# A transformer block in one kernel: squares moved from ScalarE to GpSimd, two more joint units, GpSimd's queue run by a clock

## The chip, the core and the metric

The kernel runs on one core of one Trainium2 chip. A core has five engines that run their own instruction queues and meet only through semaphores: TensorE (PE in the profile; its weight loads are PEld), VectorE (DVE), ScalarE (ACT), GpSimd (POOL) and SyncE (SP), which issues the DMAs. PE writes its results to PSUM, eight banks of 128 x 512 fp32; DVE and ACT read them there. The metric is the device time of one execution in microseconds (us), the median of several runs.

## What is computed

A pre-layernorm block: attention, then a gated feed-forward network, both with a residual. S = 2048 rows, D = 512, H = 32 heads of 16, F = 1792, all in bf16.

```python
def _A_ref(x, wqkv, wo):
    qkv = (x @ wqkv).reshape(B, S, 3, H, Dh) ...
    scores = jnp.einsum("bhqd,bhkd->bhqk", q, k) * (Dh ** -0.5)
    p = _softmax(scores, axis=-1)
    o = jnp.einsum("bhqk,bhkd->bhqd", p, v)
    return o... @ wo

def _B_ref(x, w_gate, w_up, w_down):
    return (_gelu(x @ w_gate) * (x @ w_up)) @ w_down

h = x + _A_ref(_layernorm(x), A_wqkv, A_wo)
h2 = h + _B_ref(_layernorm(h), B_w_gate, B_w_up, B_w_down)
```

The softmax takes the maximum of every row of scores, and the scores are 32 x 2048 x 2048 numbers: they are computed twice, once for the maxima and once, transposed, for the exponentials.

## The kernel before

**Units, groups and ticks.** Four heads (a slot) and 256 query rows make a unit; there are 64, and eight units (all heads for the same rows) make a group. The main loop at the end of the kernel function runs over ticks, 16 to a unit. In pass 1 a tick computes a pair of 128 x 512 score blocks (`p1_pair`, L825) and DVE reduces the pair to two maxima per row in one instruction (`p1_consume`, L840). Pass 2 follows 24 ticks behind (`P2_START`): two tiles a tick (`p2_tile`, L904), each 128 keys twice x 256 queries, and one Exp on ACT for each (`p2_consume`, L933). The exponentials wait in a ring of buffers (PTM, PTE, PTG) until `item_pv` (L947) multiplies them with the values.

**From the maxima to pass 2.** After ticks 9 and 13 of a unit `negm_part`, and after its end `negm_pre` and `negm_post` (`unit_end`), let GpSimd combine the maxima (some 17 small instructions, L851 to L876), SP transpose them (STG), and GpSimd add them to the queries (L888), so that the second scores come out with the maximum taken off. That addition is put `ADDX` = 3 ticks after the unit's end.

**Joint units.** For the units in `JOINT` (11 of them) one tick less is needed. ACT gets the difference of two score blocks (`item_diff`, L1022, L1024) and keeps its Relu in RB (L1027); DVE adds that Relu to the other block while it takes the maximum (L837, two instructions in place of one at L840), which gives the maximum of both. Tick 14 (`J_GONE`) of such a unit is left out, and pass 2's two tiles of that tick are made up on odd ticks (`behind`). `joint_prep` puts the two differences of a unit into the list `extra`; `J_PREP` says at which tick, from tick 160 at the earliest.

**Everything else goes in between.** `Dense` holds the other work of PE as generators: projections (`item_projT`, `item_projV`), values (`item_pv`), output projections (`item_oproj`), and gate, up and down of the feed-forward network. Once a tick `Dense.piece` lets the current item go on, or starts one: an extra that is due, an item of `prio` that is due, an extra, or the first of `ready`. Whether it may start hangs on `act_lag`, the planner's own account of ACT's backlog (each Exp adds 0.478, each tick takes off 1.135), and on `tight()`, which is true at the end of a joint unit. An item returns how many products of 512 columns it was worth; the loop fills a tick of pass 1 up to two with idle products (`dummy`, L1380). All of this is planned while the program is built; on the chip only the order on each engine and the semaphores count.

**Norm of the second half.** When a group's heads are done, SP transposes the rows (`post_onT`), `item_oproj` multiplies with wo, ACT adds the residual and sums the row (L1094), and two ticks later ACT squares the row with a second sum (`sq`, L1101), when its account of backlog is low. GpSimd then computes the norm (`ln2_from_sums`, `ln2_finish`, L1111 to L1125), and SP transposes it (`post_hnT`), which is done in ticks 5 to 13 of a unit alone (`clear`). Then the seven pairs of gate and up start. For each pair ACT takes both out of PSUM, GpSimd computes the inner polynomial (L1158 to L1160), ACT the Tanh (L1148; `later` waits until the backlog is under `LAG_TH` = 0.2 plus 0.02 for each tick already waited), and GpSimd the rest (L1156, L1157, L1212). The eighth group's norm and network come after both passes, in `tail_b`.

**GpSimd's queue.** `PoolStream` holds GpSimd's optional work. Each tick gives it a budget of 1.19 (at most 1.25), and the next instruction is put in the program when the budget covers its cost. `charge` keeps `t`, the time at which GpSimd would be done by the planner's clock (`TICK` = 1.135 a tick); before the change only the Tanh's placing reads it. The reciprocals of the softmax sums (`inv`, L981) are kept out of some ticks.

Of the kernel before, what the change touches and what calls it, by code (L numbers as in the profile page):

```python
# [222 lines left out]
ADDX = 3  # L223
# [7 lines left out]
TANH_LAG = 2  # L231
SLOPE = 0.02
JOINT = (12, 14, 17, 20, 25, 28, 33, 36, 41, 44, 49)
# [5 lines left out]
LAG_TH = 0.2  # L239


def bass_sequential_preLN__mha_block__geglu_ffn__prompt_kernel(nc, A_x, A_wqkv, A_wo, B_x, B_w_gate, B_w_up, B_w_down, out):
    dbg = None
    with ExitStack() as es:
# [54 lines left out]
        hn_sb = OnT[:].rearrange("p q c s -> p q (c s)")  # L299
        xres = at("xres", [128, 4, D], BF16)  # L300
# [223 lines left out]
        class Dense:  # L524
# [27 lines left out]
            def piece(self):  # L552
                if self.single and self.pause > 0:
                    return 0
                while True:
                    if self.gen is None:
                        lim = 10 ** 9
                        for it in self.prio:
                            lim = min(lim, max(it[3], self.now))
                        self.prio.sort(key=lambda it: it[3])  # L560
                        if self.extra and self.now >= 16 * self.extra[0][1][0] + 2:
                            self._start(self.extra.pop(0))
                        elif self.prio and (not self.single or self.prio[0][3] <= self.now):
                            self._start(self.prio.pop(0))
                        elif self.extra and not tight() and act_lag[0] <= LAG_EXTRA and self.now + 2 <= lim and not (self.ready and self.ready[0][0] is item_up):
                            self._start(self.extra.pop(0))
                        elif self.ready and (not self.single or ((act_lag[0] <= (-1 if tight() else LAG_START) or force[0] or self.ready[0][0] not in (item_gate, item_up)) and startable(self.ready[0], lim - self.now) and self.ready[0][3] <= self.now and self.now + self.ready[0][2] + PAUSE - 1 <= lim)):
                            self._start(self.ready.pop(0))
                        else:
                            return 0  # L570
# [46 lines left out]
        class PoolStream:  # L617

            def __init__(self):
                self.q = []  # L620
                self.budget = 0.0
                self.t = 0.0
            def add(self, ops, then=None):
                for i, (cost, fn) in enumerate(ops):
                    self.q.append((cost, fn, then if i == len(ops) - 1 else None))
                if force[0] or not ticking[0]:
                    self.run(True)
            def spend(self, cost):
                self.budget -= cost
            def charge(self, took, ready=0.0):  # L630
                self.t = max(self.t, TICK * dense.now, ready) + took
                return self.t
            def run(self, flush=False):
                while self.q and (flush or self.budget >= min(self.q[0][0], 1.0) or (self.q[0][1].__name__ == 'inv' and dense.now % 16 == 0)):
                    if not flush and self.q[0][1].__name__ == 'inv' and dense.now % 16 in (1, 2, 3, 12, 13, 14, 15):
# [242 lines left out]
        def negm_post(ui):  # L878
# [6 lines left out]
            def add():  # L885
                pool.spend(0.7)
                pool.charge(0.63, st_end[0] + 2.75)
                P.op("pool", lambda e: e.tensor_tensor(out=q_ap, in0=q_ap, in1=STG[:, par, :], op=ALU.add), reads=[("STG", par), ("qT", slot, c, hf)], writes=[("qT", slot, c, hf)])  # L888
                q_ready.add(ui)
            defer(ADDX + (ui == NU - 1), add)  # L890
# [126 lines left out]
        def item_diff(b, ui, g):  # L1017
# [11 lines left out]
            return 3  # L1029
# [33 lines left out]
        def post_onT(gi, k):  # L1063
# [7 lines left out]
            dense.add(item_oproj, gi, k, front=True, est=3, not_before=dense.now + 5)  # L1071
# [11 lines left out]
        def item_oproj(b, gi, k):  # L1083
            gp, t = gi % 2, 2 * gi + k
            hh = g_h(gi, k)
            for hc in range(4):
                P.op("pe", lambda e, hc=hc: e.matmul(pbank[:, b, :], OnT[:, k, hc, :], wo_sb[:, hc, :], start=(hc == 0), stop=False),
                     reads=[("OH", k), "wo"], writes=[("pb", b)], sig=False)
                if hc == 1:
# [5 lines left out]
                 reads=[("pb", b)], writes=[("h", gp, k), ("hsum", t)])  # L1095
            def sq():
# [7 lines left out]
            defer(2, sq)  # L1104
# [279 lines left out]
        def unit_end(ui):  # L1384
# [3 lines left out]
            negm_post(ui)  # L1388

# [5 lines left out]
        J_PREP = {max(160, 16 * (J_[i - 1] if i else 0) + 12): J_[i] for i in range(len(J_))}  # L1395
# [7 lines left out]
        while True:  # L1403
# [94 lines left out]
            if w_pieces and tick % 16 in (7, 9, 11, 13):  # L1498
# [40 lines left out]
```

## Time and profile before

| | us |
|---|---|
| median of 3 runs (1234.56 to 1235.47) | 1234.57 |
| the profiled execution | 1234.76 |
| its span, first to last instruction | 1232.9 |

The profile is one execution. Its page gives each engine's busy time and share of the span; views of the trace give the instructions in order of time (the timeline: start, length, engine, line, operation, operands, count of the instructions merged, and in brackets the idle time before it and what ended it), and busy time in chosen windows. Instructions of ACT and DVE overlap at their ends, so a full engine's pace is read from start to start, and a busy share of 99% can hide short waits. The granted TensorE clock is 1.00 in every window.

### The profile page before, as it was taken

What the parts mean: (1) busy time and instruction counts of PE and PEld (TensorE: products, weight loads), DVE (VectorE), ACT (ScalarE), POOL (GpSimd) and SP (SyncE); (2) the same over time, 40 slices, a digit from 0 to 9 for tenths busy, and PEclk for the clock granted to TensorE, in tenths of its full rate; (3) what the DMA queues carried; (4) which work ended last, traced back from release to release, by engine and by line L of the source; (5) the groups of instructions that cost most, each with busy time, mean ns of one, the idle gap of its engine ahead of it and who ended that gap; (6) DMA issues with size and microseconds to landing.
All of it is one profiled execution on the core that took longest, in us unless ns stands there. A gap on an engine that the chain in (4) does not pass through costs nothing.

```text
span 1232.9 us, 31298 instructions
## 1 busy us (share of the span) xinstructions
PE 1102.3 (89%) x12444; PEld 427.4 (35%) x12580; DVE 1179.1 (96%) x1107; ACT 1195.2 (97%) x2437; POOL 784.4 (64%) x1624
## 2 busy tenths in 40 slices
PE   7898888899999988999889998899889898888898
PEld 3233222233333333333333343333333333233335
DVE  8999999999999999999999999999999999999933
ACT  7899999999999999999999999999999999999993
POOL 8567873566756587466755677366765687347850
PEclk9999999999999999999999999999999999999999
DMA  5111113200011000100011000110001000100000
GB/s 152 27 34 30 33 50 116 76 10 9 8 27 25 8 10 9 39 13 8 11 25 27 8 8 11 25 27 8 9 10 38 14 9 8 35 17 10 8 19 14
DMA packets 68657, 31.53 MB, mean 26 GB/s; under 512 B 53920, under 2 KB 67488, under 8 KB 68512
## 3 DMA queue, kind: packets, MB, share of 16 engines
q1 hardware_dynamic: 68512, 29.52, 9.5%
q8 instruction: 101, 1.65, 0.6%
q14 instruction: 44, 0.36, 0.1%
HBM read 11.80 MB, written 2.10 MB: 11 GB/s over the span
## 4 chain that ended last, share of the span: by engine, by line
ACT 50%; DVE 30%; POOL 8%; PE 7%; issue 3%; DMA 1%; POOLq 0%; DVEq 0%
DVE PM L840 29%; ACT PTM L933 29%; ACT PTG L933 8%; ACT PTE L933 4%; PE pbank L1220 2%; ACT g_sb L669 1%; POOL th_sb L1158 1%; PE pbank L904 1%; ACT u_sb L669 1%; DMA STG<-ST 1%; PE pbank L825 1%; ACT th_sb L1148 1%; POOL LINV L981 1%; PE pbank L1168 1%; POOL GUT L1212 1%
## 5 line engine op out<-in xcount | busy, mean ns | idle before, releaser
L840 DVE TENSOR_REDUCE PM<-pbank 128x2 f32<-128x1024 f32 x1002 | 1141.4, 1213 | 8.8 <-PE pbank L904 5.1
L933 ACT ACTIVATE PTM<-pbank 128x512 bf16<-128x512 f32 x1357 | 730.3, 718 | 3.4 <-PE pbank L904 0.6
L904 PE MATMUL pbank<-QT,KT 32*128 32x256 bf16 x4096 | 512.2, 273 | 16.2 <-ACT PTM L933 6.0
L825 PE MATMUL pbank<-KT,QT 32*128 32x512 bf16 x2026 | 390.1, 384 | 29.9 <-DVE PM L840 11.3
L1380 PE MATMUL pbank<-ones_bf,ident 128*128 128x512 bf16 x697 | 217.3, 383 | 56.2 <-ACT PTM L933 29.1
L933 ACT ACTIVATE PTG<-pbank 128x512 bf16<-128x512 f32 x407 | 227.7, 716 | 1.2 <-PE pbank L904 0.2
L825 PEld LDWEIGHTS pbank<-KT,QT 32*128 32x128 bf16 x2026 | 97.7, 90 | 369.8 <-DVE PM L840 133.2
L904 PEld LDWEIGHTS pbank<-QT,KT 32*128 32x128 bf16 x4096 | 171.2, 92 | 85.2 <-ACT PTM L933 46.5
L933 ACT ACTIVATE PTE<-pbank 128x512 bf16<-128x512 f32 x236 | 139.1, 718 | 0.8
L947 PE MATMUL pbank<-PTM,VA 128*17 128x256 bf16 x2776 | 125.4, 274 | 1.5
L981 POOL TENSOR_TENSOR LINV<-OBT,negone 128x8 f32<-128x8 bf16 x62 | 103.4, 1668 | 0.0
L1380 PEld LDWEIGHTS pbank<-ones_bf,ident 128*128 128x128 bf16 x796 | 46.0, 97 | 140.1 <-ACT PTM L933 90.0
L1158 POOL TENSOR_TENSOR th_sb<-g_sb 128x512 f32<-128x512 f32 x49 | 50.9, 1040 | 41.6 <-ACT g_sb L669 41.6
L947 PEld LDWEIGHTS pbank<-PTM,VA 128*17 128x17 bf16 x2776 | 60.0, 89 | 45.7 <-issue 29.6
L1168 PE MATMUL pbank<-hnT_l,wg_sb 128*128 128x256 bf16 x448 | 67.0, 275 | 3.6
L1168 PE MATMUL pbank<-hnT_l,wu_sb 128*128 128x256 bf16 x448 | 67.1, 275 | 2.3
L868 POOL TENSOR_TENSOR MX<-PM,MX 128x8 f32<-128x8 f32 x64 | 12.8, 200 | 86.6 <-DVE PM L840 86.3
L1160 POOL TENSOR_TENSOR th_sb<-th_sb,g_sb 128x512 f32<-128x512 f32 x49 | 62.1, 1267 | 3.4
L1212 POOL TENSOR_TENSOR GUT<-th_sb,u_sb 128x512 bf16<-128x512 f32 x49 | 61.8, 1267 | 2.5
L1157 POOL TENSOR_TENSOR th_sb<-th_sb,g_sb 128x512 f32<-128x512 f32 x49 | 62.2, 1269 | 1.4
L888 POOL TENSOR_TENSOR QT<-QT,STG 128x256 bf16<-128x256 bf16 x64 | 42.7, 668 | 30.5 <-DMA STG<-ST 30.5
L1220 PE MATMUL pbank<-wd_sb,GUT 128*128 128x512 bf16 x210 | 57.3, 382 | 3.4 <-ACT OB L669 1.3
(163 smaller groups left out, 1096.0 us busy)
## 6 DMA issues: line engine op xcount, KB each, us to landing
QKS<-QKS SPq DMA_DIRECT2D x27, 112.0 KB, 2.1
x_sb<-in_A_x_dram SPq DMA_DIRECT2D x4, 512.0 KB, 5.5
xres<-in_A_x_dram SPq DMA_DIRECT2D x16, 128.0 KB, 2.3
out_dram<-out_sb SPq DMA_DIRECT2D x16, 128.0 KB, 1.7
wg_sb<-in_B_w_gate_dram SPq DMA_DIRECT2D x4, 448.0 KB, 3.6
wu_sb<-in_B_w_up_dram SPq DMA_DIRECT2D x4, 448.0 KB, 3.9
wd_sb<-in_B_w_down_dram SPq DMA_DIRECT2D x3, 512.0 KB, 4.2
STG<-ST SPq DMA_TRANSPOSE x64, 2.3
```

What stands on the lines that cost most here:

```text
L825: P.op("pe", lambda e, g=g, b=b: e.matmul(pbank[:, b, :], QT[32 * g:32 * g + 32, c, slot, 128 * qt:128 * qt + 128], KT[32 * g:32 * g + 32, ...
L840: P.op("dve", lambda e: e.tensor_reduce(out=PM[:, par, qt, kc, g:g + 2], in_=pbank[:, b:b + 2, :], axis=AX.X, op=ALU.max), reads=[("pb", b ...
L904: P.op("pe", lambda e, kt=kt, i=i: e.matmul(pbank[:, b, 256 * i:256 * i + 256], KT[32 * g:32 * g + 32, slot, 128 * kt:128 * kt + 128], QT[ ...
L933: P.op("act", lambda e, b=b, pi=pi: e.activation(out=PTt(pi), in_=pbank[:, b, :], func=ACT.Exp), reads=[("pb", b)], writes=[("PT", pi)], e ...
L947: P.op("pe", lambda e, g=g, kt=kt, pi=pi, i=i: e.matmul(pbank[32 * g:32 * g + 17, b, 0:256], VA[:, kt, 4 * slot + g, :], PTt(pi)[:, 256 * ...
L981: P.op("pool", lambda e: e.tensor_tensor(out=li, in0=o4[:, :, :, 16], in1=negone[:, 0:8].rearrange("p (q h) -> p q h", q=2), op=ALU.pow), ...
L1157: o(1.27, lambda e: e.tensor_tensor(out=ts_, in0=ts_, in1=gs, op=ALU.mult), [("th", par), ("g", par)])], then=done)
L1158: pool.add([o(1.04, lambda e: e.tensor_tensor(out=ts_, in0=gs, in1=gs, op=ALU.mult), [("g", par)], dE), o(0.62, lambda e: e.tensor_scalar( ...
L1168: P.op("pe", lambda e, dc=dc, fc=fc, i=i: e.matmul(pbank[:, b, 256 * i:256 * i + 256], w[:, dc, 128 * fc:128 * fc + 128], hT[:, dc, :], st ...
L1212: P.op("pool", lambda e: e.tensor_tensor(out=o_ap, in0=shp(ts_), in1=shp(us), op=ALU.mult), reads=[("th", par), ("u", par)], writes=o_keys ...
L1220: P.op("pe", lambda e: e.matmul(pbank[:, b, :], GUT[:, fc, 128 * k:128 * k + 128], wd_sb[:, fc, :], start=first, stop=last), reads=[("GUT" ...
L1380: P.op("pe", lambda e: e.matmul(pbank[:, b, :], ident[:], ones_bf[:, 0:512], start=True, stop=True), reads=["ident", "ones_bf"], writes=[( ...
```

## The change

Squares: for groups 0 to 5 the sum of squares is made by GpSimd: two products of 256 columns, their sum, and seven additions that halve the row, the last into `hsq`. `HQ` lies over the buffer that holds the square's output before; `HR` is new. The seventh group (`GL - 1`) keeps ACT's Square.

Two more units are joint (5 and 9), with their differences prepared from tick 60. GpSimd's queue is run by its clock from tick 64 on (`fits`): the next instruction is put in the program unless GpSimd is planned busy beyond the next tick by over 0.8, or the instruction would straddle, by over 0.3, the time at which the maxima or the addition come due. The addition is put a tick later from tick 64 on. A difference counts as one product instead of three, so that an idle one goes beside it. Differences start at a backlog of 0.05 (0.3 in the last six ticks before their unit), Tanhs at 0.05; an output projection is held back for up to six ticks while the backlog is over 0.1, and the second tile's is due one tick later; from tick 56 on projections too wait for the backlog. The weights of the feed-forward network are loaded at five ticks of a unit instead of four.

```diff
-ADDX = 3
+ADDX = 4
+CLOCK = 64
+AHEAD, OVER = 0.8, 0.3
-JOINT = (12, 14, 17, 20, 25, 28, 33, 36, 41, 44, 49)
+JOINT = (5, 9, 12, 14, 17, 20, 25, 28, 33, 36, 41, 44, 49)
-LAG_TH = 0.2
+LAG_TH = .05
...
+        HQ = at("HQ", [128, 2, 256], FP32, cur[0] - 2048)
+        HR = at("HR", [128, 256], FP32)
...
+                        elif self.prio and self.prio[0][0] is item_oproj and self.prio[0][3] <= self.now < self.prio[0][3] + 6 and act_lag[0] > 0.1:
+                            return 0
...
-                        elif self.extra and not tight() and act_lag[0] <= LAG_EXTRA and ...
+                        elif self.extra and not tight() and act_lag[0] <= (LAG_EXTRA if self.now >= 16 * self.extra[0][1][0] - 6 else 0.05) and ...
-                        elif self.ready and (... or force[0] or self.ready[0][0] not in (item_gate, item_up)) and ...
+                        elif self.ready and (... or force[0] or self.ready[0][0] not in (item_gate, item_up) and (self.ready[0][0] is not item_projT or self.now < 56)) and ...
...
+            def fits(self, took):
+                t0 = max(self.t, TICK * dense.now)
+                if t0 > TICK * (dense.now + 1) + AHEAD:
+                    return False
+                due = [TICK * (dense.now // 16 * 16 + 15) + 2.35 if dense.now < 16 * NU else 1e9]
+                if self.add_due:
+                    due.append(st_end[0] + 2.75)
+                return not any(t0 < d < t0 + took - OVER for d in due)
...
-            defer(ADDX + (ui == NU - 1), add)
+            defer(ADDX - (dense.now < CLOCK) + (ui == NU - 1), add)
...
             P.op("act", lambda e: e.activation(out=RB[:, g, :], in_=pbank[:, b, :], func=ACT.Relu), ...)
             y_left[ui] -= 1
-            return 3
+            return 1
...
-            dense.add(item_oproj, gi, k, front=True, est=3, not_before=dense.now + 5)
+            dense.add(item_oproj, gi, k, front=True, est=3, not_before=dense.now + 5 + k)
...
+            def squares():
+                hq, w = HQ[:, k, :], [("OH", k)]
+                ops = []
+                o = lambda cost, fn, reads, writes: ops.append((cost, lambda: P.op("pool", fn, reads=reads, writes=writes)))
+                o(0.63, lambda e: e.tensor_tensor(out=hq, in0=hh[:, 0:256], in1=hh[:, 0:256], op=ALU.mult), [("h", gp, k)], w)
+                o(0.63, lambda e: e.tensor_tensor(out=HR[:], in0=hh[:, 256:512], in1=hh[:, 256:512], op=ALU.mult), [("h", gp, k)], ["HR"])
+                o(0.63, lambda e: e.tensor_tensor(out=hq, in0=hq, in1=HR[:], op=ALU.add), w + ["HR"], w)
+                n = 128
+                while n > 1:
+                    o(0.2 + 0.0017 * n, lambda e, n=n: e.tensor_tensor(out=HQ[:, k, 0:n], in0=HQ[:, k, 0:n], in1=HQ[:, k, n:2 * n], op=ALU.add), w, w)
+                    n //= 2
+                o(0.2, lambda e: e.tensor_tensor(out=hsq[:, t:t + 1], in0=HQ[:, k, 0:1], in1=HQ[:, k, 1:2], op=ALU.add), w, [("hsq", t)])
+                pool.add(ops + ln2_from_sums(gi, k, t), then=lambda: defer(2, lambda: clear(lambda: post_hnT(gi, k))))
...
-            defer(2, sq)
+            defer(2, sq if gi == GL - 1 else squares)
...
-        J_PREP = {max(160, 16 * (J_[i - 1] if i else 0) + 12): J_[i] for i in range(len(J_))}
+        J_PREP = {max(60, 16 * (J_[i - 1] if i else 0) + 12): J_[i] for i in range(len(J_))}
...
-            if w_pieces and tick % 16 in (7, 9, 11, 13):
+            if w_pieces and tick % 16 in (5, 7, 9, 11, 13):
```

## The prediction

> **What bounds the kernel now.** I read the page first, then a table of windows cut at the group boundaries, then the timeline of VectorE (DVE) alone, then that of ScalarE (ACT).
>
> ```profile
> span 1232.9 us, 31298 instructions
> PE 1102.3 (89%) x12444; PEld 427.4 (35%) x12580; DVE 1179.1 (96%) x1107; ACT 1195.2 (97%) x2437; POOL 784.4 (64%) x1624
> ...
> ACT 50%; DVE 30%; POOL 8%; PE 7%; issue 3%; DMA 1%; POOLq 0%; DVEq 0%
> ```
>
> Two engines are nearly full and the chain that ends last changes between them. The profiled execution took 1234.76 us (1.9 around its span); the sum below is made against it. The median of the runs is 1234.57, 0.2 less.
>
> ```profile
> 219.37:363.50 144.13, 129.48 (x1501) 49.58 (x1515) 142.71 (x135) 143.91 (x300) 93.89 (x200) 1.00 0.09 20
> 363.50:508.37 144.87, 131.96 (x1520) 51.12 (x1535) 143.83 (x133) 144.44 (x302) 93.52 (x198) 1.00 0.07 16
> 508.37:653.40 145.03, 131.41 (x1517) 50.46 (x1534) 143.81 (x134) 144.57 (x300) 93.18 (x198) 1.00 0.07 16
> 653.40:798.27 144.87, 131.25 (x1517) 50.42 (x1532) 143.66 (x133) 144.40 (x300) 93.10 (x198) 1.00 0.07 16
> 798.27:943.30 145.03, 131.76 (x1522) 50.90 (x1539) 143.78 (x134) 144.41 (x299) 92.66 (x197) 1.00 0.08 17
> 943.30:1089.30 146.00, 130.12 (x1531) 49.79 (x1545) 145.34 (x130) 144.87 (x298) 91.85 (x194) 1.00 0.07 17
> 1089.30:1180.48 91.18, 80.24 (x960) 32.70 (x968) 90.88 (x81) 91.13 (x190) 70.81 (x140) 1.00 0.06 12
> ```
>
> Each row is a group of eight units (the last: five); the columns after the length are busy time and instructions of PE, PEld, DVE, ACT and POOL, then the granted clock. GpSimd (POOL) is busy 93 of 145 us. DVE's own pace shows in its timeline:
>
> ```profile
> 484.29 0.68 DVE L837 CUSTOM_DVE_ANT_0 OA<-pbank,OA 128x512 f32<-128x512 f32 x1
> ...
> 484.90 0.68 DVE L837 CUSTOM_DVE_ANT_0 OA<-pbank,OA 128x512 f32<-128x512 f32 x1
> ...
> 485.51 27.62 DVE L840 TENSOR_REDUCE PM<-pbank 128x2 f32<-128x1024 f32 x24
> 513.32 2.36 DVE L840 TENSOR_REDUCE PM<-pbank 128x2 f32<-128x1024 f32 x2 [0.19 <-PE pbank L904]
> 515.83 22.71 DVE L840 TENSOR_REDUCE PM<-pbank 128x2 f32<-128x1024 f32 x20
> ...
> 1009.98 145.15 DVE L840 TENSOR_REDUCE PM<-pbank 128x2 f32<-128x1024 f32 x128 [0.26 <-PE pbank L904]
> 1155.40 25.08 DVE L840 TENSOR_REDUCE PM<-pbank 128x2 f32<-128x1024 f32 x22 [0.27 <-PE pbank L904]
> ```
>
> A reduce that lasts 1.21 overlaps the next: 128 of them in 145.15 are one per (145.15 - 1.21) / 127 = 1.133 us. A joint instruction at L837 takes 0.61 (484.29 to 484.90 to 485.51). A group with two joint units has 124 reduces and four joint instructions, so DVE's floor is 124 x 1.133 + 4 x 0.61 = 142.9, and the rows say 144.9 to 145.0: about 2.1 us of stall in each of four groups. By the same count the first row (three joint units, floor 141.9) has 2.2, the sixth (none, 145.0) 1.0 and the last (80 reduces, 90.6) 0.5: **11.9 us of stall in all**. The stalls end on PE's L904, which waits for a PSUM bank, which ACT gives free: they are ACT's backlogs. Reduces end at 1155.40 + 25.08 = 1180.48; the 52 us after that are a tail.
>
> **The change part by part.**
>
> *Two more joint units* (5 and 9). Each takes out two reduces and adds two joint instructions: 2 x 1.133 - 2 x 0.61 = 1.05, for two units **-2.1**. They give ACT 2 x 2 Relus. ACT's prices, by starts in its timeline:
>
> ```profile
> 505.09 2.08 ACT L933 ACTIVATE PTG<-pbank 128x512 bf16<-128x512 f32 x4
> 507.00 0.67 ACT L1094 ACTIVATE xres<-pbank 128x512 bf16<-128x512 f32 x1
> 507.47 0.27 ACT L1094 ACTIVATION_READ_ACCUMULATOR xres<-pbank 128x1 f32 x1
> 507.57 1.16 ACT L933 ACTIVATE PTG<-pbank 128x512 bf16<-128x512 f32 x2
> 508.52 2.16 ACT L933 ACTIVATE PTM<-pbank 128x512 bf16<-128x512 f32 x4
> 510.48 0.71 ACT L1101 ACTIVATE OnT<-xres 128x512 bf16<-128x512 bf16 x1
> 511.00 0.27 ACT L1101 ACTIVATION_READ_ACCUMULATOR OnT<-xres 128x1 f32 x1
> 511.10 2.13 ACT L933 ACTIVATE PTM<-pbank 128x512 bf16<-128x512 f32 x4
> ...
> 92.74:219.37 126.63, 108.06 (x1277) 35.95 (x1290) 126.63 (x113) 124.55 (x251) 81.69 (x151) 1.00 0.21 63
> ```
>
> Four exps fill 505.09 to 507.00, 0.478 each; a Relu of the same size is put at that. The stage of units 4 to 10 (the last row) has 251 ACT instructions in 126.63: at 0.478 some 120, so 6.6 are free though the busy column hides it. Two joint units need 2 x (1.05 + 0.96) = 4.0 of that, if the rule that projections after tick 56 wait for a small backlog spreads them. Bounds -2.1 and 0 (all given back as stalls); I take -2.1.
>
> *Squares off ACT.* Twelve of fourteen go. One is 510.48 to 511.10, 0.62 with its read of the accumulator: 7.4 us of ACT, 1.24 in each of six groups. What of it is on the path is read where it stands: 24 reduces from 485.51 and two from 513.32 should take 27.2 and 2.27, and take 27.81 and 2.51, so 0.86 is lost around the two output projections (507.00 to 507.57: 0.57 each, which stay) and the two squares. I take 0.5 per group, **-3.0**; bounds 0 (the backlog is then the projections') and -0.86 x 6 = -5.2.
>
> *What GpSimd gets*: eleven instructions for each square.
>
> ```profile
> 503.86 0.20 POOL L855 TENSOR_TENSOR MX<-PM,MX 128x8 f32<-128x8 f32 x1 [3.73 <-DVE PM L840]
> 504.15 0.23 POOL L856 TENSOR_SCALAR MX<-MX 128x8 f32<-128x8 f32 x1
> ...
> 512.23 0.40 POOL L985 TENSOR_TENSOR Otok<-OBT,LINV 128x128 bf16<-128x128 bf16 x1
> 513.63 0.67 POOL L888 TENSOR_TENSOR QT<-QT,STG 128x256 bf16<-128x256 bf16 x1
> 518.63 0.77 POOL L1125 TENSOR_SCALAR OnT<-xres,rstd,nmr 128x512 bf16<-128x512 bf16 x1
> ...
> L1212 POOL TENSOR_TENSOR GUT<-th_sb,u_sb x7: 1264/1267/1268, 539.5 to 625.9; 128x512 bf16<-128x512 f32 x7
> L1094 ACT ACTIVATE xres<-pbank x2: 614/640/665, 649.5 to 652.0; 128x512 bf16<-128x512 f32 x2
> ```
>
> Three of 256 columns by L888 (3 x 0.67), one of 128 by L985 (0.40), seven of 64 down to 1 between those and L855 (about 0.22): 3.9 us by durations; starts are 0.29 apart where the row L855 says 0.20, so 4.9 with that gap. Twelve cost 47 to 59 of the 448 us that GpSimd is idle. The two tiles of a group make its norm some 10 us longer, less the gap of 3.7 at 503.86 and its like; so the feed-forward of the group starts about 8 late, or 16 where the transposes that follow the norm, which SP's queue gets in ticks 5 to 13 of a unit alone, miss a window (seven ticks). Its last product stood at 625.9 and the next output projection at 649.5, 23 us later, which hides it: 0. Without that cover the next group's products would be pushed by what is over, one for one. The seventh group, the last whose network runs in the loop, keeps its squares on ACT.
>
> The Trainium skill, "Perfetto Trace Analysis", section "GPSIMD Engine Instruction", says to time GpSimd by starts, not by reported spans; here spans give 3.9 a tile and starts 4.9, and as both lie under the cover the sum is the same by either.
>
> *GpSimd by a clock of its queue; the addition at L888 a tick later.* The order on GpSimd changes, the work does not. Behind the addition wait the gelu products of the queue; it waits for a transpose, and a tick (1.133) later more of that wait is used. The exps that need it start eight ticks after the unit. 0; in the tail, where one product of 1.27 could come ahead of it, up to +1.3.
>
> *Gates* (tanh at a backlog of 0.05 instead of 0.2, differences at 0.05, an output projection held back over 0.1, a tile's projection a tick later). They only put ACT work off to calmer ticks. The stall not counted yet is 11.9 - 5.2 = 6.7. Bounds 0 and -6.7; by nearness to the lower end (the instructions stay) **-1.0**.
>
> *A filler beside each difference.*
>
> ```profile
> 403.58 0.39 PE L825 MATMUL pbank<-KT,QT 32*128 32x512 bf16 x2
> ...
> 404.02 0.39 PE L1022 MATMUL pbank<-KT,QT 32*128 32x512 bf16 x1
> 404.25 0.37 PE L1024 MATMUL pbank<-KT,QN 32*128 32x512 bf16 x1
> 404.55 0.39 PE L825 MATMUL pbank<-KT,QT 32*128 32x512 bf16 x2
> ```
>
> A tick with a difference takes PE 0.97 (403.58 to 404.55); one more product of 0.23 (404.02 to 404.25) makes 1.20, 0.07 over the reduce. 26 of them: up to +1.8; the next ticks take it up, so 0. The weights' pieces come at five places of a unit instead of four and are needed units later: 0.
>
> **Sum**: -2.1 - 3.0 - 1.0 = -6.1; 1234.76 - 6.1 = **1228.7**.
>
> **The rivals.** *The backlog stays*: the time taken from ACT is eaten by the next burst, only the joint units count, 1232.7, or 1234.5 with the fillers' 1.8. For it: the reduces lose 0.2 to 0.3 also at places without a square (the gaps before 1009.98 and 1155.40). Against it: ACT's load falls in the very stage that loses.
>
> *ACT gets clear of DVE*: a group's floor of 142.9 is nearly reached, stalls fall from 11.9 to 3: -2.1 - 8.9, 1223.8. For it: the row 1009.98 shows 128 reduces without a gap. Against: ACT's columns stay above 144 of 145.
>
> *GpSimd is the wrong place*: if the norm slips by more than the 23 us, the squares' -3.0 is lost: 1231.7. The Trainium skill, "GPSIMD Engine Reference", section "4.1 Engine selection", speaks for this rival: elementwise products belong on VectorE, GpSimd being about twice as slow. In this trace VectorE is the engine without room and GpSimd is idle a third of the time, so I give it little.
>
> *The slower one: the tanhs of the seventh group.* A tanh may start at a backlog of 0.05, and the limit rises by 0.02 a tick: where ACT never calms down it waits up to 7.5 ticks, 8.5 us, until the old 0.2. Two buffers alternate over seven pairs, so 3.5 such waits stand in a row.
>
> ```profile
> 1188.02 1.28 POOL L1212 TENSOR_TENSOR GUT<-th_sb,u_sb 128x512 bf16<-128x512 f32 x1
> ...
> 1203.76 1.28 ACT L1322 ACT_TABLE_LOAD   x1
> ```
>
> The last product of that group stands at 1188.0 and the exps end at 1203.8; with some 6 for the down projections (28 products at 0.23) 10 us are covered. At six ticks a wait (6.8) the chain slips by 24, 14 over: 1242.7. It decides from a slip of 16 (10 and the 6.1 won). Against it: the same tanhs now find their places while ACT is full.
>
> **How the numbers follow.** What a measurement of this kernel can tell from no change is about 0.2%, 2.5 us. Forecast 0.59 (own range 1225.5 to 1231.5, nearly all faster), backlog stays 0.17 (same), ACT clear 0.10 (faster), wrong place 0.04 (just faster), seventh group's tanhs 0.10 (slower). Faster 0.70, with a part of the forecast and of the wrong place counted as same: 0.19; slower 0.11. The range 1224.0 to 1235.0 takes in the backlog case with the fillers and most of the clear case; the tail of both and the slow rival stay out.
>
> **What would show it.** Joint units: 998 reduces and 26 joint instructions, units 5 and 9 about 17.1 long. Squares: only the seventh group's two left on ACT, and the stretch after the output projections of a group 0.5 shorter per 26 reduces. Groups of two joint units near 144.3 instead of 145.0. GpSimd near 840 busy, the first product of a group some 8 later. Gates: fewer gaps before L840 in the feed-forward units. A tail still 52 long speaks against the slow rival. I am wrong if group lengths stay at 145 (backlog), or if the reduces end earlier and the kernel does not.

## The result and the profile after

The changed kernel takes 1231.15 us (median of 8 runs, 1230.68 to 1231.70); the kernel before took 1234.82 in the same comparison (8 runs, 1234.56 to 1235.47). The ratio is 0.997, with a 95% interval of 0.9959 to 0.998: faster by 0.3%, a little more than the 0.2% that the prediction takes for the smallest change that a measurement tells, and 2.5 us less of a gain than the forecast of 1228.7. By the time alone the rival "GpSimd is the wrong place" (1231.7) lies nearer; which terms came out has to be read from the traces and the runs. The profiled execution of the changed kernel took 1231.23, with a span of 1229.3.

The head of its page: span, then busy time, share and instructions of each engine.

```profile
span 1229.3 us, 31435 instructions
...
PE 1104.8 (90%) x12462; PEld 429.5 (35%) x12598; DVE 1175.8 (96%) x1111; ACT 1189.5 (97%) x2417; POOL 834.6 (68%) x1760
...
L856 DVE TENSOR_REDUCE PM<-pbank 128x2 f32<-128x1024 f32 x998 | 1135.9, 1212 | 8.3 <-PE pbank L921 3.8
```

ACT lost 5.7 us of busy time, GpSimd gained 50, and 998 reduces are left. The windows, cut at the same places of the program as before (columns as there):

```profile
217.97:361.97 144.00, 129.23 (x1508) 49.42 (x1523) 142.74 (x136) 143.29 (x293) 100.05 (x220) 1.00 0.10 24
361.97:506.32 144.35, 130.97 (x1522) 50.47 (x1536) 143.45 (x134) 143.61 (x296) 101.24 (x220) 1.00 0.07 16
506.32:650.68 144.36, 131.07 (x1522) 50.46 (x1536) 143.46 (x134) 143.61 (x296) 101.26 (x220) 1.00 0.07 16
650.68:795.04 144.36, 131.09 (x1522) 50.48 (x1536) 143.46 (x134) 143.61 (x296) 101.26 (x220) 1.00 0.08 16
795.04:939.51 144.47, 130.58 (x1522) 50.39 (x1536) 143.34 (x133) 143.69 (x296) 100.71 (x219) 1.00 0.07 16
939.51:1085.29 145.78, 129.84 (x1534) 50.24 (x1548) 145.14 (x130) 143.63 (x296) 101.86 (x218) 1.00 0.08 18
1085.29:1176.84 91.55, 81.22 (x961) 33.22 (x971) 91.08 (x81) 91.47 (x191) 68.72 (x137) 1.00 0.06 12
```

The four groups of 144.9 to 145.0 are now 144.35 to 144.47, each 0.5 to 0.7 shorter. The first group gained 0.13, the sixth 0.22, and the last row, which was 91.18, lost 0.37. So the gain a group was about what was forecast, and the last two rows took little part in it.

To follow this unit by unit, take from each of the 64 units its own floor (16 reduces by 1.1335, or 14 reduces and two joint instructions by 0.609). What is left is its stall; below, units are counted from 0, and "stall from unit 11" is the sum over units 11 to 63. It was 11.41 before and is **9.21** after. From the first reduce's start to the last one's end it was 1165.81 and is 1161.51: **-4.30**, of which -2.10 are the two joint units and -2.20 stall. The tail behind the last reduce is 52.45 where it was 52.44.

DVE's timeline in the third group shows where the stall went:

```profile
483.05 18.45 DVE L856 TENSOR_REDUCE PM<-pbank 128x2 f32<-128x1024 f32 x16
501.78 34.03 DVE L856 TENSOR_REDUCE PM<-pbank 128x2 f32<-128x1024 f32 x30 [0.28 <-PE pbank L921]
...
536.94 87.90 DVE L856 TENSOR_REDUCE PM<-pbank 128x2 f32<-128x1024 f32 x77
625.05 1.23 DVE L856 TENSOR_REDUCE PM<-pbank 128x2 f32<-128x1024 f32 x1 [0.21 <-PE pbank L921]
...
627.41 18.45 DVE L856 TENSOR_REDUCE PM<-pbank 128x2 f32<-128x1024 f32 x16
646.14 14.79 DVE L856 TENSOR_REDUCE PM<-pbank 128x2 f32<-128x1024 f32 x13 [0.28 <-PE pbank L921]
```

The 30 reduces from 501.78 lie around both output projections and the place where the squares stood. They take 34.03, and 29 x 1.1335 + 1.21 is 34.08: not a trace of the old 0.86 is left. But 16 reduces from 627.41 to 646.14, just before the next output projections, take 18.73 where 18.14 is the floor; before, the same 16 took 18.19. GpSimd's last gelu products and ACT's output projections stand there:

```profile
L1242 POOL TENSOR_TENSOR GUT<-th_sb,u_sb x7: 1263/1265/1272, 572.1 to 648.7; 128x512 bf16<-128x512 f32 x7
...
L1111 ACT ACTIVATE xres<-pbank x2: 603/604/604, 651.2 to 655.7; 128x512 bf16<-128x512 f32 x2
```

The first product of the group came at 572.1 instead of 539.5 and the last at 648.7 instead of 625.9. The cover of 23 us ahead of the output projections (now at 651.2) has shrunk to 2.5.

A second new place is units 57 to 59, which stall 0.25, 0.44 and 0.34; before, they had none. DVE's timeline shows two gaps there:

```profile
1057.62 22.71 DVE L856 TENSOR_REDUCE PM<-pbank 128x2 f32<-128x1024 f32 x20 [0.20 <-PE pbank L921]
1080.72 15.16 DVE L856 TENSOR_REDUCE PM<-pbank 128x2 f32<-128x1024 f32 x13 [0.39 <-PE pbank L921]
```

The first costs 0.28 and follows a late addition to QT. The view of the STG transposes from 1040 to 1090 (durations as least, median, most in ns; then who waited) and PE's timeline:

```profile
L898 SPq DMA_TRANSPOSE STG<-ST x3: 1170/1177/2051, 1053.1 to 1087.4; - x3
...
  PE pbank L841: 1.0, 1
```

```profile
1057.19 0.39 PE L841 MATMUL pbank<-KT,QT 32*128 32x512 bf16 x2 [1.02 <-POOL QT L905]
```

One transpose lasted 2.05 us instead of 1.17, the addition at L905 came that much later, and the second pass's scores (L921), issued in one group with those of L841, waited 1.02 for it. The second gap costs 0.47 and stands at the seventh group's first output projection, which waited for the transposes of the heads' output (OnT), the longest of them 1.83:

```profile
L1084 SPq DMA_TRANSPOSE OnT<-Otok x2: 1194/1514/1834, 1074.1 to 1076.5; - x2
...
  PEld pbank L1104: 1.4, 1
```

```profile
1079.98 0.38 PE L1104 MATMUL pbank<-wo_sb,OnT 128*128 128x512 bf16 x1 [1.36 <-ACT PTG L950]
```

The other 0.3 lies at that group's second output projection (1086.5 to 1089.0), and no wait in the views explains it.

### The profile page after: what moved, and what is told of

It is laid out like the page before. It is cut to its first block, busy times and chain, and to the rows that moved or that the text cites. A ratio compares the mean times of both kernels' runs of the same rounds, so it can differ in the third digit from the quotient of the medians.

```text
span 1229.3 us, 31435 instructions
## 1 busy us (share of the span) xinstructions
PE 1104.8 (90%) x12462; PEld 429.5 (35%) x12598; DVE 1175.8 (96%) x1111; ACT 1189.5 (97%) x2417; POOL 834.6 (68%) x1760
## 4 chain that ended last, share of the span: by engine, by line
ACT 57%; DVE 29%; PE 8%; issue 3%; POOL 2%; DMA 0%; POOLq 0%; DVEq 0%
ACT PTM L950 32%; DVE PM L856 29%; ACT PTG L950 10%; ACT PTE L950 6%; PE pbank L1250 2%; ACT g_sb L685 2%; ACT u_sb L685 2%; ACT th_sb L1178 2%; PE pbank L841 1%; PE pbank L921 1%; PE pbank L1198 1%; ACT OB L685 1%; PE pbank L443 1%; DVE OA L853 1%; PE pbank L1410 1%
## 5 line engine op out<-in xcount | busy, mean ns | idle before, releaser
L921 PE MATMUL pbank<-QT,KT 32*128 32x256 bf16 x4096 | 503.0, 273 | 14.8 <-ACT PTM L950 7.6
L841 PE MATMUL pbank<-KT,QT 32*128 32x512 bf16 x2022 | 388.6, 384 | 31.5 <-DVE PM L856 11.8
L1410 PE MATMUL pbank<-ones_bf,ident 128*128 128x512 bf16 x708 | 221.4, 384 | 52.2 <-ACT PTM L950 22.5
L950 ACT ACTIVATE PTG<-pbank 128x512 bf16<-128x512 f32 x407 | 224.8, 704 | 1.7 <-PE pbank L921 1.3
L841 PEld LDWEIGHTS pbank<-KT,QT 32*128 32x128 bf16 x2022 | 97.9, 90 | 363.4 <-DVE PM L856 139.0
L921 PEld LDWEIGHTS pbank<-QT,KT 32*128 32x128 bf16 x4096 | 170.3, 92 | 75.9 <-ACT PTM L950 40.4
L905 POOL TENSOR_TENSOR QT<-QT,STG 128x256 bf16<-128x256 bf16 x64 | 42.8, 669 | 23.0 <-DMA STG<-ST 22.3
L1186 POOL TENSOR_SCALAR th_sb<-th_sb 128x512 f32<-128x512 f32 x49 | 30.4, 620 | 39.7 <-ACT th_sb L1178 39.7
```

The costliest lines, as they stand in the source:

```text
L841: P.op("pe", lambda e, g=g, b=b: e.matmul(pbank[:, b, :], QT[32 * g:32 * g + 32, c, slot, 128 * qt:128 * qt + 128], KT[32 * g:32 * g + 32, ...
L921: P.op("pe", lambda e, kt=kt, i=i: e.matmul(pbank[:, b, 256 * i:256 * i + 256], KT[32 * g:32 * g + 32, slot, 128 * kt:128 * kt + 128], QT[ ...
L950: P.op("act", lambda e, b=b, pi=pi: e.activation(out=PTt(pi), in_=pbank[:, b, :], func=ACT.Exp), reads=[("pb", b)], writes=[("PT", pi)], e ...
L1410: P.op("pe", lambda e: e.matmul(pbank[:, b, :], ident[:], ones_bf[:, 0:512], start=True, stop=True), reads=["ident", "ones_bf"], writes=[( ...
```

## The experiments

Each run's median is given with its ratio to the kernel before of the same comparison; "reduces" is the time from the first reduce's start to the last one's end in its profiled execution. Several of them have a stretch of 3.41 us at half the TensorE clock in the profiled execution, told of in the last section; where a unit's stall contains one it is said, since it isn't the edit's price. In the 14 profiled executions a granted clock of 1.000 goes with no such stretch in the loop and a lower one with one or two, so the clock recorded for the other executions tells which of them had one.

### The squares back on ACT

```
-            defer(2, sq if gi == GL - 1 else squares)
+            defer(2, sq)
```

> The changed kernel with all squares back on ACT, the rest of the change kept. Its reduces take 1161.5 us from the first start to the last end in the changed kernel, 1165.8 in the one before. Theory (the squares' relief is real, but the longer norm on GpSimd lets the feed-forward network start 25 us later and its last units lose what was won): the network of groups 1 to 4 starts 10 or more us earlier than in the changed kernel (836 for group 4 instead of 845), 0.4 to 0.6 of stall per group comes back behind the output projections, 0.3 or more goes away in the last two units of the network, and the reduces take 1162 to 1163.5. Rival (forecast: squares are worth 0.5 a group and nothing is paid for the slip): 1164.5, with the last units of the network unchanged. Rival (squares do nothing, the gates do it): 1161.5.

1234.82 us (1233.23 to 1237.08), ratio 0.9998 (0.9988 to 1.0007); reduces 1166.17, stall 13.86. Units 57 to 59 hold 3.1 of it, where the changed kernel has 1.0: some 0.9 is half clock in unit 57, the rest stands at late transposes of STG and OnT, for which PE waited 1.6 and 1.8. The first five groups stall 9.66 where the changed kernel has 7.66, 0.40 a group, and units 51 to 54 have 0.39 instead of -0.14. So the move is worth **2.0 + 0.53 = 2.5** here. The medians differ by 3.7, and the five executions at a clock of 1.000 (median 1234.0) from the changed kernel's five (1230.8) by 3.2; these take in units 57 to 59, so 2.5 is a low reading. But the network did not come back:

```profile
L1242 POOL TENSOR_TENSOR GUT<-th_sb,u_sb x7: 1263/1266/1277, 573.1 to 649.7; 128x512 bf16<-128x512 f32 x7
```

573.1 to 649.7 with the squares on ACT, 572.1 to 648.7 without. That part of the expectation is wrong: in this program the slip of the network is not the squares' doing alone. Nor is it a late norm. The transposes behind the norm (hnT_l) and the down projections of the group before (wd_sb), in the kernel before, in the changed one and in this run:

```profile
L1077 SPq DMA_TRANSPOSE hnT_l<-OnT x2: 1190/1192/1195, 516.3 to 519.4; - x2
L1220 PE MATMUL pbank<-wd_sb,GUT x26: 379/379/390, 508.3 to 525.9; 128*128 128x512 bf16 x26
```

```profile
L1094 SPq DMA_TRANSPOSE hnT_l<-OnT x2: 1194/1230/1265, 519.8 to 530.7; - x2
L1250 PE MATMUL pbank<-wd_sb,GUT x26: 379/379/390, 524.0 to 548.4; 128*128 128x512 bf16 x26
```

```profile
L1094 SPq DMA_TRANSPOSE hnT_l<-OnT x2: 1190/1192/1195, 512.2 to 518.2; - x2
L1250 PE MATMUL pbank<-wd_sb,GUT x26: 379/379/390, 521.7 to 549.3; 128*128 128x512 bf16 x26
```

With the squares on ACT the norm is as early as before, and the first gate product still comes at 554.9, where it came at 528.0 before and at 554.0 in the changed kernel: the down projections stand ahead of it. Which of the other edits puts them there no run shows.

### The squares alone, in the kernel before

The function squares() and its two buffers are put into the kernel before, and nothing else:

```
-            defer(2, sq)
+            defer(2, sq if gi == GL - 1 else squares)
```

> The kernel before with the squares of twelve tiles as eleven GpSimd instructions each, nothing else changed. Theory A (the network slips): the stall at the two squares of a group goes (about 0.8 a group), but the first gelu product of a group starts 15 to 25 us later and the last one ends within 5 us of the next output projections, so the units there gain 0.5 to 0.8 a group of new stall, and waits for OnT of 4 us and more appear at the output projections; the reduces end within 1 of the kernel before (165.8 in 1165.8 from first start to last end: 1165.0 to 1167.0), time 1234 to 1236. Theory B (as predicted): the cover of 23 us holds, the reduces take 3.0 less, 1162.8, time 1231.8.

1236.55 us (1233.99 to 1238.00), ratio 1.0009 (1.0000 to 1.0018); reduces 1167.50, of which 2.0 are half clock in unit 52. Without that 1165.5: the change's largest term brings **0.3 when it comes alone**. The waits (us in total, times, longest) and the network's last products:

```profile
PEld pbank L1089 <- DMA OnT<-Otok: 5.4, 4, 1.6
...
PE pbank L1089 <- DMA OnT<-Otok: 1.3, 1, 1.3
```

```profile
L1227 POOL TENSOR_TENSOR GUT<-th_sb,u_sb x7: 1262/1268/1272, 574.8 to 658.9; 128x512 bf16<-128x512 f32 x7
...
L1096 ACT ACTIVATE xres<-pbank x2: 606/634/662, 654.5 to 657.0; 128x512 bf16<-128x512 f32 x2
```

Here the last product is at 658.9, behind the output projections at 654.5: the cover is used up, GpSimd has the last products and the heads' output to make in the same stretch, and PE waits 6.7 us for the transposes of the heads' output, where it waited 0.5 before; a group earlier they go out at 505.1 instead of 494.5. Theory A holds, but for the first product, which comes 35 us later instead of the 15 to 25 it expected.

### GpSimd's queue without its clock

```
-CLOCK = 64
+CLOCK = 10 ** 9
```

This also puts the addition back to three ticks, and keeps the reciprocals out of some ticks again.

> The changed kernel with GpSimd's queue run by the old budget to the end (and the addition at 3 ticks). Theory (the clock changes the order on GpSimd and hardly the time): the reduces take 1161.0 to 1162.5, the tail stays at 52.4, the network's start moves by less than 5 us. Rival (the clock is what delays the network): it starts 10 us or more earlier, and the reduces take 1160 or less. Rival (the clock is the gain): 1163.5 or more.

1234.45 us (1233.11 to 1236.45), ratio 0.9995 (0.9986 to 1.0005); reduces 1164.29. Units 18, 26, 34 and 42, the first of each group's output projections, stall 1.35, 1.50, 1.21 and 1.30 instead of 0.60 each (unit 27's 0.90 is a half clock).

```profile
PEld pbank L1104 <- DMA OnT<-Otok: 6.9, 4, 1.8
PE pbank L1104 <- DMA OnT<-Otok: 4.4, 3, 1.5
```

The waits are of the kind that the squares alone have, and with the clock the changed kernel has 1.4 in all. So the clock, priced at nothing, is what makes the late network bearable: 2.8 us of the reduces, some 0.9 of it half clock, and against it stands the changed kernel's 1.0 in units 57 to 59, which this execution doesn't have.

### Without the gates

The tanh's limit is 0.2 again, extras start at 0.3, no output projection is held back, no tile's projection put off, and projections after tick 56 do not wait:

```
-LAG_TH = .05
+LAG_TH = 0.2
...
-                        elif self.prio and self.prio[0][0] is item_oproj and self.prio[0][3] <= self.now < self.prio[0][3] + 6 and act_lag[0] > 0.1:
-                            return 0
...
-            dense.add(item_oproj, gi, k, front=True, est=3, not_before=dense.now + 5 + k)
+            dense.add(item_oproj, gi, k, front=True, est=3, not_before=dense.now + 5)
```

> The changed kernel with the gates of before: tanh at a backlog of 0.2, differences at 0.3, output projections not held and the second tile's not put off, projections after tick 56 not held. Theory (forecast: the gates are worth about 1.0): the reduces take 1162.5, with more and smaller gaps in the network's units. Rival (all that the stalls fell comes from the gates): 1163.7. Rival (the gates delay the network and cost): 1161 or less, the network starting 5 us or more earlier.

1231.84 us (1231.15 to 1232.50), ratio 0.9975 (0.9966 to 0.9984); reduces 1162.53, **+1.02**. Units 4 to 6 stall 0.35, 0.07 and 0.33 where there was none, and a steady group 1.53 instead of 1.37. Units 57 to 59 stall 0.33 here instead of 1.04, so up to unit 56 the gates are worth 1.7: 0.75 beside joint unit 5, and 0.8 in units 11 to 56. In time they are worth 0.7 by the medians and 0.9 at a clock of 1.000, so the forecast's size is about right.

### Eleven joint units, and two joint units alone

```
-JOINT = (5, 9, 12, 14, 17, 20, 25, 28, 33, 36, 41, 44, 49)
+JOINT = (12, 14, 17, 20, 25, 28, 33, 36, 41, 44, 49)
```

The differences are again prepared from tick 160 at the earliest.

> The changed kernel with the eleven joint units of before. Theory: units 5 and 9 take 18.1 us again instead of 17.06, the rest is the same to 0.2, and the reduces take 1163.6. Rival (the two units load ACT before the network begins and cost later): less than 1163.0.

1234.07 us (1232.60 to 1236.41), ratio 0.9994 (0.9984 to 1.0004); reduces 1164.76, with 2.40 in unit 58, where PE waited 2.09 for OnT's transposes and half clock followed: 1162.3 without. The changed kernel less its 1.0 in units 57 to 59 stands at 1160.4. The difference of 1.9 is the forecast's 2.1.

In the kernel before, units 5 and 9 are made joint units, with their differences prepared from tick 60, and nothing else:

```
-JOINT = (12, 14, 17, 20, 25, 28, 33, 36, 41, 44, 49)
+JOINT = (5, 9, 12, 14, 17, 20, 25, 28, 33, 36, 41, 44, 49)
```

> The kernel before with units 5 and 9 as joint units and nothing else changed. Theory A: each takes 1.05 off DVE and ACT has the room, so the reduces take 1163.7 from first start to last end (-2.1) and the median is 1232.5 to 1233. Rival: without the calmer gates ACT falls behind in the stage of units 4 to 10 and gives back 1 us or more there: 1164.8 or more.

1234.25 us (1233.89 to 1235.40), ratio 0.9994 (0.9985 to 1.0004); reduces 1165.35, -0.46. Units 4, 5, 6 and 10 stall 0.35, 0.07, 0.33 and 0.24 where they had none, and units 28 and 50 another 0.25 and 0.71. The rival holds: 1.0 is given back beside the two units, 0.75 of it just as in the run without the gates. That units 28 and 50, far from them, stall another 0.96 isn't explained.

### No filler beside the differences

```
-            return 1
+            return 3
```

> The changed kernel with a difference counted as three products again (no filler beside it). Theory A: the fillers cost and bring nothing on DVE's side, reduces within 0.5 of the changed kernel's 1161.5, time 1231.0 to 1231.7. Rival: the fillers' 0.07 a time were paid, 1.8 less: 1159.7, time 1229.4. Second rival: they keep PE's 3.4 us windows full, and without them one or more windows of half clock appear, each 1 to 2.5 longer.

1231.79 us (1229.40 to 1238.43), ratio 0.9977 (0.9963 to 0.9992); stall 9.63, of which 1.6 is half clock in units 27, 43 and 44: 8.0, against 8.2 of the changed kernel without its units 57 to 59. So by theory A the fillers cost DVE nothing outside units 57 to 59, and the second rival is right too: without them the clock falls twice in the profiled execution. Single executions spread over 9 us; the changed kernel's over 1. But the three executions at a clock of 1.000 take 1229.40, 1229.47 and 1229.52, the first rival's number, where the changed kernel's five take 1230.68 to 1231.23. So at full clock the kernel is some 1.3 faster without the fillers; in the profiled execution units 57 to 59 stall nothing, which would be most of it. Whether the fillers bring that stall about no run shows.

### The joint units moved

```
-JOINT = (5, 9, 12, 14, 17, 20, 25, 28, 33, 36, 41, 44, 49)
+JOINT = (5, 9, 12, 14, 17, 20, 28, 29, 36, 37, 44, 45, 49)
```

> The changed kernel with joint units 28, 29, 36, 37, 44, 45 in place of 25, 28, 33, 36, 41, 44 (still 13). Theory A (the late end of the network lies over joint units 25, 33, 41 and is what stalls 24-26, 32-34, 40-42 by 1.1 to 1.2 a group): those stalls fall by 0.5 to 0.8 a group, and if two joint units in a row cost less than that, the reduces take 1160 to 1161, time 1230. Rival (the stall belongs to the network's end whatever unit it lies over): 24-26 and the like keep 0.9 or more, and the two joint units in a row add stall at 29, 37, 45: reduces 1162 to 1163.5, time 1232 or more.

1231.02 us (1230.69 to 1232.70), ratio 0.9968 (0.9956 to 0.998); reduces 1161.30. Where units 24 to 26 lose their joint unit, the last product comes at 497.8, 5.4 ahead of the output projections at 503.2, and the three stall 0.13 in all instead of 1.23. But later groups stall 0.45 in unit 29 and 0.56 in unit 32 and the like, 1.35 a group as against 1.37 in the changed kernel. With the second joint unit of a pair one later still:

```
-JOINT = (5, 9, 12, 14, 17, 20, 25, 28, 33, 36, 41, 44, 49)
+JOINT = (5, 9, 12, 14, 17, 20, 28, 30, 36, 38, 44, 46, 49)
```

> The changed kernel with joint units 28, 30, 36, 38, 44, 46 in place of 25, 28, 33, 36, 41, 44 (still 13): as in the run with 28, 29 and the like the network's end keeps clear of a joint unit, and the second joint unit comes after the network's first pairs. Theory A (ACT's backlog after two joint units in a row is what kept 29 and 32 at 0.45 and 0.56): those fall below 0.3, a group stalls 0.8 to 1.0 instead of 1.37, reduces 1159.5 to 1160.3, time 1229.5. Rival (a group gives ACT the same work wherever the joint units stand, and it stalls what it lacks): 1.3 to 1.4 a group, reduces 1161 to 1162, time 1231.

1231.14 us (1230.04 to 1232.66), ratio 0.9969 (0.9959 to 0.998); reduces 1162.80, of which about 1.9 are half clock in units 0 and 58; another 1.07 in unit 58 stands at OnT's transposes, ahead of the fall of the clock. The three groups from unit 19 stall 0.26, 1.51 and 0.94. Both runs end between theory A and the rival: units 11 to 56 stall 6.7 and 6.8 instead of 7.6, so the move wins 0.8 to 0.9 there, and the medians show at most 0.1 of it.

### No run past the maxima

```
-AHEAD, OVER = 0.8, 0.3
+AHEAD, OVER = 0.8, 0.0
```

> The changed kernel with OVER = 0: no piece of GpSimd's queue may run past the time of the maxima or of the addition. Theory A (the stalls of units 57 to 59, 1.0 in all, come from an addition that is late since the maxima were): the transposes of STG are issued up to 0.3 earlier, the wait of PE's L841 for QT goes, units 57 to 59 stall below 0.3 in all, reduces 1160.8. Rival (the late addition is a transpose that lasts 2.05 instead of 1.17, whatever the queue does): units 57 to 59 keep 0.5 or more, and the network slips a little further, reduces 1161.5 or more.

1232.67 us (1231.91 to 1233.15), ratio 0.998 (0.9971 to 0.999); reduces 1159.08, **-2.43**, and units 57 to 59 stall 0.15 in all. Unit 56's transpose goes out 3.3 behind the unit's end instead of 4.8 and takes 1.17, and PE does not wait for OnT. That fits theory A, and the gain is larger than expected; that the transposes were not long in this execution by chance, one execution can't rule out. But the kernel is slower by 1.5: the tail is **56.32** instead of 52.45. The last product of the seventh group stands at 1197.1, 23.2 after the last reduce, in the changed kernel at 1185.6, 8.8 after it. A slip of 14.4 costs 3.9, so 10.5 of it are covered.

### Fifteen joint units, and an earlier start

```
-JOINT = (5, 9, 12, 14, 17, 20, 25, 28, 33, 36, 41, 44, 49)
+JOINT = (5, 7, 9, 12, 14, 17, 20, 25, 28, 33, 36, 41, 44, 49, 53)
```

> The changed kernel with units 7 and 53 as joint units too (15). Theory A (where a stage's units show no stall, ACT has room, and a joint unit brings its 1.05): units 3 to 10 and 51 to 54 show none in the changed kernel, so the reduces take 1159.4 (-2.1) and the median is about 1229.1. Rival (ACT's backlog is only just cleared there): units 8 and 9 or 54 to 56 stall by 0.5 or more each, the reduces take 1160.5 or more, time 1230.2 or more.

1230.55 us (1229.84 to 1231.50), ratio 0.9965 (0.9952 to 0.9978); reduces 1157.46, **-4.05**, of which 2.1 are the joint units; units 8, 9 and 54 to 56 stall 0.32 at most. The network, one pair of products a unit instead of two in places, spreads over more units and a group stalls 1.12. And 3.9 of the 4.05 go in the tail, 56.33:

```profile
L1242 POOL TENSOR_TENSOR GUT<-th_sb,u_sb x7: 1267/1272/1278, 1130.6 to 1196.1; 128x512 bf16<-128x512 f32 x7
```

With the same joint units, gate and up products are now let in at a backlog of 0.4:

```
-LAG_START = 0.3
+LAG_START = 0.4
```

> The changed kernel with joint units 7 and 53 too, and gate and up products allowed to start at a backlog of 0.4 instead of 0.3, so that in the order of the program the network of groups 1 to 4 starts and ends about three units earlier than in the run with 7 and 53 alone (last product in the place 33.7 instead of 36.6), ahead of the next output projections again, and the seventh group's last product is at 64.4 instead of 65.2. Theory A (the tail grew by 3.9 there because the seventh group's network ended 14 later against the reduces, 10 of them covered): the tail is 52.4 again; with the reduces at 1157 to 1158 the time is 1226.5 to 1227.5. Rival (the start at a larger backlog is paid on VectorE): groups stall 1.5 or more instead of 1.12, reduces 1159.5 or more, time 1228.5 or more.

1229.67 us (1229.28 to 1231.38), ratio 0.9959 (0.9944 to 0.9973).

```profile
L1242 POOL TENSOR_TENSOR GUT<-th_sb,u_sb x7: 1266/1268/1280, 1117.0 to 1184.9; 128x512 bf16<-128x512 f32 x7
```

The tail is 52.45 again, as theory A says, but the reduces take 1162.49 (1.0 of it half clock in unit 0), as the rival says, though a steady group stalls less than its 1.5: units 11 to 26 stall 5.6 instead of 3.1. The network's last product stands in unit 33 again, some 20 us ahead of the output projections, and a steady group stalls 1.27: the cover, given back, buys nothing on DVE here. This is the lowest median of the study; its interval overlaps the changed kernel's, so the two aren't told apart by it.

## Why the prediction was right, and where its sum was off

The direction and the range held; the sum of -6.1 came out as -3.5 in the profiled executions. The range takes in two of the rivals' times too (1231.7 and 1232.7), so the time alone doesn't speak for the forecast; the groups of 144.4, forecast as 144.3, do. By its own terms:

- **Two joint units, -2.1**: right in size (1.9 by the run with eleven, 2.1 by the floor). That ACT has the room was right only with the gates; in the kernel before the reduces gain 0.46.
- **Squares, -3.0**: 2.5 by the units, 3.2 by the executions at a clock of 1.000. A steady group gave 0.40 by the run that takes them back, with 0.5 forecast. The row it was read from was the right one: the 0.86 is gone there, and part of it stands again before the next output projections.
- **GpSimd's longer norm, 0, hidden by 23 us**: the step that failed in its reasoning. The product was to be 8 late, or 16; the first was 33 late and the last 23. The norm itself is as late as forecast: the second tile's transposes go out at 530.7 instead of 519.4, 11 later. What was not foreseen is that the down projections of the group before, which end at 548.4 instead of 525.9, go ahead of the gate products, and do so with the squares on ACT too. The price of nothing was nearly right for a reason that the prediction did not have: the clock of GpSimd's queue. In the kernel before, which lacks it, the squares bring 0.3, which is the rival "GpSimd is the wrong place" with its mechanism. With it the cover was down to 2.5, so the term came out by luck.
- **The clock, 0**: some 2.8 in the company of the squares, the largest miss of a single term; it keeps the squares' gain; what it does alone no run shows.
- **The addition, 0 in the loop**: 0.28 in the profiled execution, by a transpose of 2.05. The other 0.8 of the 1.0 in units 57 to 59 stands at the seventh group's output projections, which the sum did not look at. The runs without fillers and without the clock show none of the 1.0.
- **Gates, -1.0**: 1.0 by the reduces of the run without them, 1.7 up to unit 56. It was counted as stall taken from the feed-forward units; that is 0.8 of it, and 0.75 is what keeps units 4 to 6 clear.
- **Fillers, 0**: right for the units up to 56. What they do for the clock was not seen, nor that executions at full clock are 1.3 faster without them.
- **The tail, 52 long**: right. The slower rival's mechanism exists: its 10 us of cover were 10.5 in the two kernels in which the seventh group slipped. In the changed kernel that group ended 8.8 behind the last reduce, near the 7.5 of before (1188.0 against 1180.5), so the rival had nothing to charge.

Added up: -2.1 and -2.5, with +1.0 for units 57 to 59, are -3.6; the gates' 0.75 at units 4 to 6 is inside the joint units' term. The reduces show -4.3, and the 0.7 that is left is about the gates' 0.8 in units 11 to 56, though parts taken out one at a time need not add up. Of the -4.3, 0.65 is missing at the start of the profiled execution: its first reduce stands at 15.32, before at 14.67, while both programs issue the same work there. The medians differ by 3.67.

## What to carry to other kernels

When work is moved to an engine with idle time, price the order in which that engine takes it up: here the same eleven instructions for a square were worth 0.3 us in the kernel before and 2.5 in the changed one, and the run without the clock puts most of the difference down to a queue that keeps clear of the two pieces that others wait for. A cover read from one trace (23 us) is used up by the other edits of the same change, so it is worth asking of each of them what it makes later. And where a loop's stall falls, look at the tail before counting the gain: twice a loop shorter by 2.4 and 4.05 gave 3.9 back behind its last reduce.

## What the hardware showed beside that

**One thin window is enough to halve the TensorE clock.** The rows are windows of the run with eleven joint units and of the run without fillers (PE busy time and count come first; the clock is the third column from the end).

```profile
1074.40:1077.80 3.40, 3.27 (x68) 1.51 (x66) 3.40 (x4) 3.40 (x8) 0.64 (x3) 1.00 0.40 108
1077.80:1081.20 3.40, 1.52 (x36) 0.61 (x28) 3.40 (x4) 3.05 (x7) 0.00 (x0) 1.00 0.54 93
1081.20:1084.60 3.40, 2.89 (x16) 0.69 (x17) 1.36 (x2) 1.36 (x3) 2.76 (x6) 0.50 0.09 18
```

```profile
804.18:807.59 3.41, 2.88 (x61) 1.18 (x52) 3.41 (x4) 3.29 (x8) 2.67 (x13) 1.00 0.00 0
807.59:811.00 3.41, 2.80 (x24) 0.91 (x24) 3.41 (x4) 3.41 (x8) 3.15 (x6) 1.00 0.23 45
811.00:814.41 3.41, 3.41 (x18) 0.67 (x19) 2.87 (x4) 2.78 (x6) 2.68 (x14) 0.50 0.09 17
```

In the first, PE waited 2.09 us for OnT's transposes and was busy 1.52 of 3.40; then its clock stood at 0.50 for 3.41 us, and the unit stalled 2.40. In the second PE's timeline shows no gap over 0.4 us and it was busy 2.80 of 3.41, but of the 22 products that start in the window 20 had operands of 32 rows, and the clock fell all the same: this is the stretch that the fillers fill in the changed kernel.

All nine such stretches in the profiled executions of this study begin at a whole number of 3.413 us after the moment at which the clock first went full: in the first run 1075.2 after it, 315 x 3.413. In the changed kernel PE is busy only 2.00 of the 3.41 us from 1077.2 and keeps its clock; counted from its own first full clock, two windows share that stretch, busy 2.75 and 2.56. So it seems to be chance whether a thin stretch falls into one such window; no run here shifted the grid on purpose. Busy time alone doesn't decide either, since 2.80 was too little in the second case above. The Trainium skill, "TensorE: Matmul & The Clock Gate", Part 1, gives a free-running window of 3413 ns, and the traces agree. Its table under "Why this matters for your kernels" allows idle gaps of up to about 3 us, and here a gap of 2.09, and a window with none over 0.4, were enough.

The same moment seems to set the start: over the 14 profiled executions the clock first goes full between 5.0 and 7.8 us, and the first reduce stands between 14.66 and 15.49, at 14.67 where it was 5.0 and at 15.32 where it was 7.4. That is 0.6 us between two executions which no edit explains.
